# A batch's 6080 tokens cut into pairs of chunks of 512 and 504, in place of 512 and 480

## The chip, the cores and the metric

The kernel runs on one core of one Trainium2 chip. The metric is the device time of one execution in microseconds (us). The core has a matrix engine (TensorE, PE in the profile, with its weight loads as PEld), a vector engine (VectorE, DVE), an activation engine (ScalarE, ACT), GpSimd (POOL), and SyncE (SP), from whose queue all transfers are issued here.

## The reference

```python
def _attn_ref(q, k, v, tau):            # (4, 6080, 256) each
    qn = q / (np.linalg.norm(q, axis=1, keepdims=True) + 1e-06)
    kn = k / (np.linalg.norm(k, axis=1, keepdims=True) + 1e-06)
    s = kn.transpose(0, 2, 1) @ qn / tau
    s = s - s.max(-1, keepdims=True)
    a = np.exp(s)
    a /= a.sum(-1, keepdims=True) + 1e-09
    return v @ a

def _moe_ref(x, w_in, w_out):           # (24320, 256), (256, 2048), (2048, 256)
    h = x @ w_in
    g = h - np.tanh(h)
    return g @ w_out
```

The attention is over channels: for each of 4 batches a 256 x 256 matrix `a` is made from all 6080 tokens, and `v @ a` goes through a two-layer network with 2048 hidden units. All is float32.

## The kernel before, in words

**Folding.** Since `(v @ a) @ w_in = v @ (a @ w_in)`, the kernel multiplies `a` into `w_in` once a batch, and then streams the tokens of `v` through the folded weights `f`. A slot is one slice of 256 hidden units (there are 8 slices, `NS2`) against one pair of token chunks. The batch's tokens are cut into 6 pairs (L255 to L260): a pair takes `2 * n` tokens, `n` for each of its two chunks, with `n` at most 512 (`NMAX`). That gives five pairs of n = 512 and a last one of n = 480. A batch has 48 slots, and the 4 batches have 192.

**A slot.** Two chunks by two halves of the channels by two halves of the slice make a 2 x 2 block product, which is done in Strassen's way with 7 products, p1 to p7 (`Quad`, L965), into the PSUM banks x, y and z. Each number is held as a high part in float32r and a low part, and each product is three matmuls, high by low, high by high, low by high (`products`, L294 to L304; the matmul is at L300). So a slot has 21 matmuls of n columns here. ScalarE copies intermediate sums out (u, p at L999), VectorE adds them (c at L1015), and `finish` makes `h - tanh(h)` and splits it: tanh on ScalarE (L1027), the subtraction on VectorE (L1031), the high part gh on ScalarE (L1035), the low part gl on VectorE (L1039).

**The second layer.** `second` (L1077) multiplies each of the slot's four blocks by `w_out` in 6 matmuls (L1099), 24 in a slot, adding up over the 8 slices into the banks ps_o. After a pair's last slice the sums are copied out (ob, L1118) and stored (L1121).

**Beside it.** While one batch streams, the next batch's scores are built up from float32r matmuls of 256 columns (ps_s), in the batch's second to fifth pair; in its last pair come the softmax, and the fold of `a` into `w_in`, whose matmuls have 512 columns (x and z from wt). The first batch has its own scores, softmax and fold ahead, up to about 79 us. `Moving` (L775) loads a pair's tokens (vraw, L788), forms the sums that Strassen's products need (L795, L798) and splits them into high and low parts (L807, L810). These tiles are allotted at the full 512 whatever `n` is.

**What sets the order.** `Plan` (L85) collects all operations with costs in us and dependencies, and `order` places them: TensorE's in the order in which they were added, the others' by earliest start, then due time. The cost of a matmul is `pe_cost(n)` = 0.0134 + 0.000417 n. The outer loop (L1360) walks the slots and adds their products by the table `ORDER`; the second layer's matmuls are drawn from a stream that lags some 30 matmuls behind (`LAG`, `drain`, L1344). The host lays out the tokens pair by pair in the same cut (L1416 to L1419).

Of the kernel before, what the change touches and what calls it, by code (L numbers as in the profile page):

```python
# [18 lines left out]
P = 128  # L19
GJ = 2  # L20
NMAX = 512
NSQ = 760
F64_SCALE = 2.0 ** -112

# [210 lines left out]
def pe_cost(n):  # L235
    return 0.0134 + n * 0.000417


@with_exitstack
def attn_moe(ctx: ExitStack, tc: tile.TileContext, qk, v4, qkT, tau, w_in, w_out, outT):  # L240

# [6 lines left out]
    B, N, _, C = qk.shape  # L248
# [3 lines left out]
    FB = 2 * P  # L252
    NJ = N // P
    TAIL = N - NJ * P
    pairs = []  # L255
    s0 = 0
    while s0 < N:
        n = min(NMAX, (N - s0) // 2)
        pairs.append((s0, n))
        s0 += 2 * n  # L260
    NP = len(pairs)
    SLOTS = NP * NS2
    TOTAL = B * SLOTS
# [18 lines left out]
    def sb(pool, tag, shape, dtype, name):  # L282
        return pool.tile(list(shape), dtype, tag=tag, name=name, bufs=ring[tag].bufs)

    def bank(i, name, shape=(P, 512)):

        return ps_p.tile(list(shape), F32, tag=f"bank{i}", name=name)
# [38 lines left out]
    class Convert:  # L326
# [10 lines left out]
        def magnitude(self):  # L337
            words = self.raw.rearrange("p a (n w) -> p (a n) w", w=2)
            self.low, self.high = words[:, :, 0], words[:, :, 1]
            self.a = sb(nt_p, "nt", [P, NSQ], I32, f"a_{self.name}")[:, 0:WN]  # L340
            self.af = self.a.bitcast(F32)
# [98 lines left out]
    while j < NJ:  # L440
        n = min(GJ, NJ - j) if j else NJ % GJ or GJ
# [7 lines left out]
    class Attn:  # L449
# [26 lines left out]
        def square_plain(self, g):  # L476
            j0, n, rows = groups[g]
            raw = self.parts[g]
            if g == 0:

                self.acc = [bank(i, f"acc{i}_{self.b}", (P, 2, C)) for i in (4, 3)]
                self.acc.append(sb(g_p, "t", [P, NMAX], F32, "acc").rearrange("p (x c) -> p x c", x=2))
                for a in self.acc[n:]:
# [41 lines left out]
        def split_hi(self, g):  # L525
            j0, n, rows = groups[g]
            raw = self.parts[g][0]
            hi = sb(qk_p, "qh", [P, GJ, 2, C], F32R, f"qh_{self.b}_{g}")
            nc.scalar.copy(hi[:rows, 0:n], raw[:rows, 0:n])
            self.parts[g] = [hi, raw]  # L530
# [26 lines left out]
        def load_channels(self, i):  # L557

            row, part = divmod(i, N // NSQ)
            self.channels[i] = sb(nt_p, "nt", [P, NSQ], F32, f"nt_{self.b}_{i}")  # L560
            nc.sync.dma_start(
                self.channels[i],
                qkT[row // KC, self.b, row % KC * P:(row % KC + 1) * P, part * NSQ:(part + 1) * NSQ],
            )

        def square(self, i):
            if i == 0:
                self.squares = sm_p.tile([P, 2 * KC, N // NSQ], F32, name="squares")
            x = self.channels.pop(i)
            row, part = divmod(i, N // NSQ)  # L570
            nc.scalar.activation(x, x, AF.Square, accum_out=self.squares[:, row, part:part + 1])
# [203 lines left out]
    class Moving:  # L775
# [9 lines left out]
        def load(self):  # L785
            n, s0 = self.n, self.s0
            self.raw = sb(v_p, "vraw", [P, 4, NMAX], F32, f"vraw_{self.b}_{self.p}")
            nc.sync.dma_start(self.raw[:, :, 0:n], v4[self.b, :, 2 * s0:2 * s0 + 4 * n].rearrange("p (a n) -> p a n", a=4))  # L788

        def sums(self, i):  # L790
            n = self.n
            r = self.raw[:, :, 0:n]
            if i == 0:
                self.t = sb(v_p, "vt", [P, 4, NMAX], F32, f"vt_{self.b}_{self.p}")
                nc.vector.tensor_sub(self.t[:, 0:2, 0:n], r[:, 1:3, :], r[:, 0:2, :])  # L795
# [8 lines left out]
        def split_hi(self, i):  # L804
            x = sb(v_p, "vhl", [P, 2, NMAX], F32R, f"v{i}_{self.b}_{self.p}")
            self.hi[i], self.lo[i] = (x[:, j, 0:self.n] for j in range(2))
# [52 lines left out]
    def plan_product(b, q, p, z):  # L859
# [10 lines left out]
        ps = a.banks[to]  # L870
        plan.add("PE", 3 * pe_cost(NMAX), lambda to=to: a.fold_product(q, to, z, i, x, first), reads=[fbufs.pop((b, q, x)), a.ebuf] + [a.shbuf] * (i >= S1), writes=[ps])

# [487 lines left out]
    for gs in range(TOTAL):  # L1360
# [3 lines left out]
        for name, then in ORDER:  # L1364
# [6 lines left out]
            for x in then:  # L1371
                if isinstance(x, int):
                    lag, x = max(0, lag - x), max(0, x - lag)
# [68 lines left out]
```

## Time and profile before

| what | value |
|---|---|
| time, median of 3 runs | 2155.19 us (2155.01 to 2155.44) |
| span of the profiled execution, first to last instruction | 2154.0 us |
| instructions | 28464 |
| moved by DMA | 357.97 MB, mean 166 GB/s |

The profile gives the profiled execution by its span alone; it lies 1.2 us below the median, which also holds what is around the span. Four views are used. The page has the busy time of each engine and the chain of work that ended last. The groups list instructions of one line, operation and shape, with their number, busy time and mean duration of one; behind the last bar stand the engine's idle time just before them and what ended it. The timeline has one row for each run of like instructions: start in us, time from the first start to the last end, engine, line, tiles, shape and number. The windows give, for a stretch of time, its length and then the busy time and number of instructions of PE, PEld, DVE, ACT and POOL, the granted clock, and the DMA's share and rate.

Matmuls are pipelined: a matmul's duration in a row reaches past the start of the next one, so that TensorE's rate is read from the distance between starts.

### The profile page before, as it was taken

The numbers are of one execution on the slowest core, as the hardware profiler recorded it, in microseconds if no ns is written. First come the engines' busy times: TensorE is split into PE (matmuls) and PEld (weight loads), VectorE is DVE, ScalarE is ACT, GpSimd is POOL, SyncE is SP. The second block draws the span as 40 slices with busy tenths as digits, with TensorE's granted clock in tenths as the row PEclk, the third lists the DMA queues.
The fourth block names the chain that finished last, engine by engine and source line by source line (L and its number), as shares of the span: only waits on it lengthen the run. The fifth ranks groups of instructions, "written<-read, shape, count | busy, mean of one in ns | idle before, by whom it ended". The sixth has DMA issues, their size and how long they took to land.

```text
span 2154.0 us, 28464 instructions
## 1 busy us (share of the span) xinstructions
PE 2147.9 (100%) x9908; PEld 1805.5 (84%) x9908; DVE 1780.1 (83%) x2928; ACT 1540.0 (71%) x2762; POOL 34.8 (2%) x31
## 2 busy tenths in 40 slices
PE   9999999999999999999999999999999999999999
PEld 8888888888888888888888888888888888888888
DVE  8998878878888778787889877878788978778776
ACT  6677777767777777776777877777677766666665
POOL 5100000000000000000000000000000000000000
PEclk9999999999999999999999999999999999999999
DMA  9845556535335454543533555454353332332331
GB/s 382 304 162 203 187 208 217 181 128 183 133 134 201 164 206 168 209 160 111 193 137 124 187 193 206 145 215 166 107 193 129 142 131 88 140 125 86 131 115 53
DMA packets 97505, 357.97 MB, mean 166 GB/s; under 512 B 9938, under 2 KB 27346, under 8 KB 94802
## 3 DMA queue, kind: packets, MB, share of 16 engines
q1 hardware_dynamic: 97362, 356.16, 45.9%
q8 instruction: 78, 1.28, 0.2%
q14 instruction: 65, 0.53, 0.1%
HBM read 293.47 MB, written 62.65 MB: 165 GB/s over the span
## 4 chain that ended last, share of the span: by engine, by line
PE 99%; DMA 0%; SPq 0%; ACT 0%; issue 0%
PE ps_o L1099 48%; PE x L300 25%; PE y L300 12%; PE ps_s L300 7%; PE z L300 7%; PE ps_w L300 1%; DMA vhl<-qk_dram 0%; PE ps_b L613 0%; PE ps_t L648 0%; SPq L514 0%; SPq L335 0%; PE ps_n L506 0%; ACT ob L1118 0%; SPq L1291 0%; PE ps_tau L316 0%
## 5 line engine op out<-in xcount | busy, mean ns | idle before, releaser
L300 PE MATMUL x<-v,f 128*128 128x512 f32 (+1 forms) x2304 | 613.4, 388 | 0.0
L1099 PE MATMUL ps_o<-gh,wo_h 128*128 128x512 f32 (+1 forms) x1536 | 596.0, 388 | 0.0
L1099 PE MATMUL ps_o<-gh,wo_l 128*128 128x512 f32 (+1 forms) x1536 | 595.4, 388 | 0.0
L1039 DVE TENSOR_TENSOR gl<-t,gh 128x512 fp32r<-128x512 f32 (+1 forms) x768 | 510.2, 681 | 99.9 <-ACT gh L1035 94.2
L1035 ACT CAST gh<-t 128x512 fp32r<-128x512 f32 (+1 forms) x768 | 461.0, 617 | 125.4 <-DVE t L1031 110.0
L300 PEld LDWEIGHTS x<-v,f 128*128 128x128 f32 x2304 | 432.5, 188 | 87.0
L1027 ACT ACTIVATE t<-c 128x512 f32<-128x512 f32 (+1 forms) x576 | 361.5, 628 | 162.4 <-DVE c L1015 156.4
L1099 PE MATMUL ps_o<-gl,wo_h 128*128 128x512 f32 (+1 forms) x1536 | 471.6, 388 | 0.0
L1031 DVE TENSOR_TENSOR t<-c,t 128x512 f32<-128x512 f32 (+1 forms) x576 | 392.0, 682 | 94.8 <-ACT t L1027 87.8
L1099 PEld LDWEIGHTS ps_o<-gl,wo_h 128*128 128x128 f32 x1536 | 288.3, 188 | 57.9
L1099 PEld LDWEIGHTS ps_o<-gh,wo_l 128*128 128x128 f32 x1536 | 288.5, 188 | 55.7
L1099 PEld LDWEIGHTS ps_o<-gh,wo_h 128*128 128x128 f32 x1536 | 288.5, 188 | 55.5
L300 PE MATMUL y<-v,f 128*128 128x512 f32 (+1 forms) x1152 | 321.7, 387 | 0.0
L999 ACT COPY u<-x 128x512 f32<-128x512 f32 (+1 forms) x384 | 223.4, 582 | 128.5 <-PE x L300 125.7
L1015 DVE TENSOR_TENSOR c<-u,y 128x512 f32<-128x512 f32 (+1 forms) x384 | 260.0, 677 | 35.7 <-PE y L300 21.3
L300 PEld LDWEIGHTS y<-v,f 128*128 128x128 f32 x1152 | 216.2, 188 | 43.4
L1027 ACT ACTIVATE t<-x 128x512 f32<-128x512 f32 (+1 forms) x192 | 113.7, 592 | 111.8 <-PE x L300 111.1
L1031 DVE TENSOR_TENSOR t<-x,t 128x512 f32<-128x512 f32 (+1 forms) x192 | 131.2, 683 | 61.0 <-ACT t L1027 60.6
L1015 DVE TENSOR_TENSOR c<-p,z 128x512 f32<-128x512 f32 (+1 forms) x192 | 130.4, 679 | 37.1 <-PE z L300 34.4
L300 PE MATMUL z<-v,f 128*128 128x512 f32 (+1 forms) x576 | 160.8, 387 | 0.0
L300 PEld LDWEIGHTS z<-v,f 128*128 128x128 f32 x576 | 108.1, 188 | 21.6
L999 ACT COPY p<-x 128x512 f32<-128x512 f32 (+1 forms) x192 | 111.6, 581 | 3.0 <-PE x L300 0.9
(161 smaller groups left out, 1516.7 us busy)
## 6 DMA issues: line engine op xcount, KB each, us to landing
f<-f_d SPq DMA_DIRECT2D x160, 896.0 KB, 4.6
nt<-qkT_dram SPq DMA_DIRECT2D x96, 380.0 KB, 5.8
f_d<-f SPq DMA_DIRECT2D x32, 896.0 KB, 4.0
raw<-qk_dram SPq DMA_DIRECT2D x52, 512.0 KB, 5.8
vraw<-v_dram SPq DMA_DIRECT2D x20, 1024.0 KB, 7.8
outT_dram<-ob SPq DMA_DIRECT2D x80, 256.0 KB, 4.2
wt<-wt_d SPq DMA_DIRECT2D x24, 512.0 KB, 6.7
wt<-wi_d SPq DMA_DIRECT2D x36, 256.0 KB, 5.1
```

Of the source, the lines that this page charges most:

```text
L300: ins = nc.tensor.matmul(out, w, x, start=first and i == 0, stop=last and i == len(seq) - 1, skip_group_check=True,)
L999: nc.scalar.copy(self.tiles[to], self.tiles["X"][:, 0:self.n])
L1015: nc.vector.tensor_add(self.tiles[i], self.tiles[u], self.tiles[ps][:, 0:self.n])
L1027: nc.scalar.activation(self.tiles["t", i], self.tiles[c][:, 0:n], AF.Tanh)
L1031: nc.vector.tensor_sub(x, self.tiles[c][:, 0:n], x)
L1035: nc.scalar.copy(self.g[i][0], self.tiles["t", i])
L1039: nc.vector.tensor_sub(self.g[i][1], self.tiles["t", i], self.g[i][0].bitcast(F32))
L1099: nc.tensor.matmul(outs[key + (m,)][:, 0:n], (wo_l if part else wo_h)[:, f, m * P:(m + 1) * P], quad.g[i][x], start=first and j == 0, stop ...
```

## The change

The loop that cut off 512 after 512 is replaced by a function that divides a batch's tokens as evenly as steps of 8 allow, with the same number of pairs. For 6080 tokens: `count` = 6, `each` = 63, `more` = 2, so two pairs of n = 64 x 8 = 512 and four of n = 63 x 8 = 504. The host uses the same function for its layout.

```diff
+UNIT = 8
...
+def token_pairs(N):
+
+    count = -(-N // (2 * NMAX))
+    each, more = divmod(N // (2 * UNIT), count)
+    pairs = []
+    s0 = 0
+    for p in range(count):
+        n = UNIT * (each + (p < more))
+        pairs.append((s0, n))
+        s0 += 2 * n
+    assert s0 == N and pairs[0][1] <= NMAX
+    return pairs
...
-    pairs = []
-    s0 = 0
-    while s0 < N:
-        n = min(NMAX, (N - s0) // 2)
-        pairs.append((s0, n))
-        s0 += 2 * n
+    pairs = token_pairs(N)
...
-    for s0 in range(0, N, 2 * NMAX):
-        x, y = np.split(vT[:, :, s0:s0 + 2 * NMAX], 2, axis=2)
+    for s0, n in token_pairs(N):
+        x, y = np.split(vT[:, :, s0:s0 + 2 * n], 2, axis=2)
```

The lines of the changed kernel are 10 further down (L300 becomes L310, L1099 becomes L1109). On TensorE, in the last batch's fifth pair (x, y of pair 4, slices 6 and 7, with the second layer of slice 5), before:

```order
L300 MATMUL x_4_6_20299<-v_3_4_19712,f_20151 128x512 x3
L300 MATMUL x_4_7_20389<-v_3_4_19357,f_20246 128x512 x3
L1099 MATMUL ps_o_4_1_1_19923<-gh_3_4_5_20313,wo_h 128x512
L300 MATMUL y_4_6_20353<-v_3_4_19739,f_20151 128x512 x3
L1099 MATMUL ps_o_4_1_1_19923<-gl_3_4_5_20324,wo_h 128x512
L1099 MATMUL ps_o_4_1_0_19918<-gl_3_4_5_20324,wo_h 128x512
```

and at the same place now:

```order
L310 MATMUL x_4_6_20299<-v_3_4_19712,f_20151 128x504 x3
L310 MATMUL x_4_7_20389<-v_3_4_19357,f_20246 128x504 x3
L1109 MATMUL ps_o_4_1_1_19923<-gh_3_4_5_20313,wo_h 128x504
L310 MATMUL y_4_6_20353<-v_3_4_19739,f_20151 128x504 x3
L1109 MATMUL ps_o_4_1_1_19923<-gl_3_4_5_20324,wo_h 128x504
L1109 MATMUL ps_o_4_1_0_19918<-gl_3_4_5_20324,wo_h 128x504
```

Only the number of columns differs, and so it is over the whole of TensorE's program, 6822 rows in both. On ScalarE, in the first batch's third pair (pair 2, slices 2 and 3; p, u, t and gh as above, nt the squares for the next batch's norms), before:

```order
L1027 ACTIVATE t_0_2_2_2816<-x_2_2_2701 128x512
L571 ACTIVATE nt_14_2765,squares<-nt_14_2765 128x760
L999 COPY p_0_2_3_2826<-x_2_3_2812 128x512
L1035 CAST gh_0_2_2_2832<-t_0_2_2_2810 128x512
L1035 CAST gh_0_2_2_2838<-t_0_2_2_2816 128x512
```

and now:

```order
L1037 ACTIVATE t_0_2_2_2816<-x_2_2_2701 128x504
L1009 COPY p_0_2_3_2823<-x_2_3_2812 128x504
L581 ACTIVATE nt_14_2765,squares<-nt_14_2765 128x760
L1045 CAST gh_0_2_2_2833<-t_0_2_2_2810 128x504
L1045 CAST gh_0_2_2_2838<-t_0_2_2_2816 128x504
```

The copy of p and the squares have changed places. Such swaps of neighbours are found in ScalarE's, VectorE's and SyncE's programs from the third pair on.

## The prediction

> **What bounds the kernel now.** I read the page from the top: busy shares, then the chain that ended last, then the granted clock.
>
> ```profile
> PE 2147.9 (100%) x9908; PEld 1805.5 (84%) x9908; DVE 1780.1 (83%) x2928; ACT 1540.0 (71%) x2762; POOL 34.8 (2%) x31
> PE 99%; DMA 0%; SPq 0%; ACT 0%; issue 0%
> core 0: 2154.0 us, clock 1.000
> ```
>
> TensorE is the chain from end to end, at a full granted clock. The other engines wait for it, not it for them. So the time is the sum of the spacings from one matmul's start to the next one's, and the question is what one matmul of 504 columns costs. A matmul's own duration in the groups (about 390 ns) does not say it, because matmuls overlap; the spacing has to be taken from the timeline.
>
> The work comes in slots: one pair of chunks against one 256-wide slice of the hidden layer. By the code a slot has 7 products of 3 matmuls and 24 matmuls of the second layer, 45 in all. The groups kept apart by shape bear that out for the sixth pair (4 batches x 8 slots = 32 slots):
>
> ```profile
> L300 PE MATMUL x<-v,f 128*128 128x480 f32 x384 | 99.4, 378 | 0.0
> L1099 PE MATMUL ps_o<-gh,wo_h 128*128 128x480 f32 x256 | 97.2, 380 | 0.0
> L1099 PE MATMUL ps_o<-gh,wo_l 128*128 128x480 f32 x256 | 96.6, 377 | 0.0
> L1099 PE MATMUL ps_o<-gl,wo_h 128*128 128x480 f32 x256 | 76.5, 379 | 0.0
> L300 PE MATMUL y<-v,f 128*128 128x480 f32 x192 | 51.9, 378 | 0.0
> L300 PE MATMUL z<-v,f 128*128 128x480 f32 x96 | 26.0, 379 | 0.0
> ```
>
> They add up to 1440 = 32 x 45, and the last column says that TensorE was never idle ahead of one. A slot's period can be read off its z product, which comes once a slot. In the last batch, where nothing else is inserted, TensorE's timeline has it at these starts (first column, us), six slots apart at 512 columns and four slots apart at 480:
>
> ```profile
> 1709.59 0.84 PE L300 MATMUL z<-v,f 128*128 128x512 f32 x3
> ...
> 1770.79 0.84 PE L300 MATMUL z<-v,f 128*128 128x512 f32 x3
> ...
> 2086.48 0.81 PE L300 MATMUL z<-v,f 128*128 128x480 f32 x3
> ...
> 2125.48 0.81 PE L300 MATMUL z<-v,f 128*128 128x480 f32 x3
> ```
>
> At 512 a slot takes 61.20 / 6 = 10.20 us, at 480 it takes 39.00 / 4 = 9.75 us. Divided by 45, a matmul starts every **226.7 ns** at 512 columns and every **216.7 ns** at 480. A third size stands in the scores of the earlier batches, 256 columns:
>
> ```profile
> 1003.81 0.28 PE L300 MATMUL ps_s<-ql,qh 128*128 128x256 f32 x1
> 1003.93 0.28 PE L300 MATMUL ps_s<-qh 128*128 128x256 f32 x1
> 1004.05 0.28 PE L300 MATMUL ps_s<-qh,ql 128*128 128x256 f32 x1
> 1004.17 0.40 PE L1099 MATMUL ps_o<-gh,wo_l 128*128 128x512 f32 x1
> ```
>
> Three in 0.36 us, so 120 ns each. These three sizes do not lie on a line. From 256 to 512 the price is 106.7 ns for 256 columns, 0.4167 ns a column, and 13.3 ns a matmul beside it. On that line 480 columns would cost 213.3 ns and a slot 9.60 us; the trace has 9.75. **The 480 size pays 3.3 ns a matmul, 0.15 us a slot, above the line that 256 and 512 lie on.** Everything hangs on whether 504 pays that too.
>
> **The change, part by part.** Columns are conserved: a batch's halves are 5 x 512 + 480 = 3040 before and 2 x 512 + 4 x 504 = 3040 now. The number of matmuls, of slots and of instructions on every engine stays, and TensorE's order stays row for row apart from the sizes. Per run that is 24 pairs x 8 = 192 slots. Before, 160 of them are 512 and 32 are 480: 160 x 10.20 + 32 x 9.75 = 1944.0 us. Now 64 are 512 and 128 are 504: 652.8 + 128 x s, with s the slot at 504. So the change costs nothing at s = 1291.2 / 128 = 10.0875 us, and each 0.01 us of s is worth 1.28 us.
>
> No row of this trace has 504 columns, so s is bounded from both sides. Lower end: the line through 256 and 512 gives 226.67 - 8 x 0.4167 = 223.33 ns, s = 10.05 us, and the change saves 128 x 0.0375 = **4.8 us**. Middle: the line through 480 and 512, the two nearest sizes, gives 224.2 ns, s = 10.0875 us, and by construction exactly **nothing**. Upper ends: if 504 pays what 480 pays, 223.33 + 3.33 = 226.67 ns, s = 10.20 us, the same slot as at 512, and the change costs 128 x 0.1125 = **14.4 us**. If it pays more, the dearest run of spacings that I find without a wait is that of 512-column matmuls just behind three of 480:
>
> ```profile
> 502.31 0.40 PE L1099 MATMUL ps_o<-gh,wo_h 128*128 128x512 f32 x1
> ...
> 504.39 0.39 PE L1099 MATMUL ps_o<-gh,wo_h 128*128 128x512 f32 x1
> ```
>
> Nine matmuls of 512 stand in those 2.08 us, 231.1 ns each, 4.4 ns above their settled 226.7. With 4.4 ns on the line 504 would cost 227.8 ns, s = 10.25 us, and the change 20.7 us.
>
> I take 14.4 us, for what these rows say about the kind of price. The sizes 256 and 512 settle into an even beat; 480 does not:
>
> ```profile
> 1100.27 0.37 PE L1099 MATMUL ps_o<-gh,wo_l 128*128 128x480 f32 x1
> 1100.48 0.38 PE L1099 MATMUL ps_o<-gh,wo_h 128*128 128x480 f32 x1
> 1100.70 0.37 PE L1099 MATMUL ps_o<-gh,wo_l 128*128 128x480 f32 x1
> 1100.91 0.38 PE L1099 MATMUL ps_o<-gh,wo_h 128*128 128x480 f32 x1
> 1101.13 0.59 PE L1099 MATMUL ps_o<-gl,wo_h 128*128 128x480 f32 x2
> ```
>
> The spacings alternate, 0.21 and 0.22 us: every second one stands on the line, and the next pays for both. Behind an odd number of 480s (three, above) the following 512s are late for some nine matmuls. Behind an even number they are not:
>
> ```profile
> 505.07 0.81 PE L300 MATMUL x<-v,f 128*128 128x480 f32 x3
> 505.72 0.82 PE L300 MATMUL z<-v,f 128*128 128x480 f32 x3
> 506.38 0.39 PE L1099 MATMUL ps_o<-gh,wo_l 128*128 128x512 f32 x1
> ...
> 507.28 0.81 PE L300 MATMUL y<-v,f 128*128 128x480 f32 x3
> ```
>
> Six of 480, then four of 512 in 0.90 us, 225 ns each, settled at once. Something keeps step with the columns, 512 and 256 leave it in step, and 480 puts it half out and then back in. 504 is as little in step with 512 or 256 as 480 is, so I expect it to pay on average, and the nearest measured average is 480's 3.3 ns. That step, from 480 to 504, is the weak one.
>
> The other terms are small. Slots in which two sizes are mixed cost a little more than their parts:
>
> ```profile
> 2066.57 0.81 PE L300 MATMUL z<-v,f 128*128 128x480 f32 x3
> ...
> 2076.65 0.81 PE L300 MATMUL z<-v,f 128*128 128x480 f32 x3
> ```
>
> This slot takes 10.08 us, where 21 matmuls of 480 and 24 of 512 would make 21 x 0.2167 + 24 x 0.2267 = 9.99. Before and now there are seven such changes of size (one within each batch, one between batches), with two mixed slots each at most; at 0.09 us that is 7 x 0.18 = 1.3 us, which I leave where it is and keep as a margin either way. VectorE and ScalarE follow the columns:
>
> ```profile
> L1118 ACT COPY ob<-ps_o 128x512 f32<-128x512 f32 x40 | 23.4, 586 | 7.3 <-PE ps_o L1099 6.6 <-DMA outT_dram<-ob 0.5
> L1118 ACT COPY ob<-ps_o 128x480 f32<-128x480 f32 x8 | 4.5, 559 | 4.4 <-PE ps_o L1099 4.3
> 520.00:583.00 63.00, 63.00 (x293) 54.24 (x292) 52.47 (x102) 43.35 (x79) 0.00 (x0) 1.00 0.51 180
> 90.00:176.00 86.00, 86.00 (x409) 72.34 (x408) 84.39 (x152) 65.53 (x121) 3.27 (x2) 1.00 0.50 185
> ACT v L807 <- DMA vraw<-v_dram: 1.7, 1, 1.7
> ```
>
> The copy that ends the program grows by 27 x 24/32 = 20 ns, the only certain gain or loss behind the last matmul. In the sixth pair (second-to-last window row, the columns being length, then PE, PEld, DVE, ACT) VectorE is busy 52.5 of 63 us; its operations there grow by 5%, about 2.6 us, under cover of the 10.5 us that it is idle. The one stretch where VectorE has no slack, 84.4 of 86 us, is the first pair of the first batch, which stays at 512. The new tokens were waited for once, 1.7 us at the start; the loads shrink or grow by at most 5%. Swaps in ScalarE's and SyncE's order are between neighbours. I cost all this at nothing; were TensorE made to wait 0.1 us in each of the 128 slots, it would be 12.8 us.
>
> **Sum.** The profiled execution has a span of 2154.0 us, 1.2 us below the median of 2155.19; I carry that difference over. 2154.0 + 14.4 = 2168.4 us of span, **2169.6 us** of time, 0.7% slower.
>
> **Rivals.** *The straight line holds (faster).* 480's 3.3 ns would then be no matter of step but a floor under the spacing, near 216.7 ns, that 512 and now 504 clear. It decides from the point where the line passes the floor, (216.7 - 13.3) / 0.4167 = 488 columns: 504 is above it, so s = 10.05 us and the time is 2155.2 - 4.8 = 2150.4 us. For it: 480 keeps about the same mean in two batches, 0.86 us for the four spacings that alternate above and 216.7 ns each in the last pair. Against it: the 256s above run at 120 ns, well under such a floor; and 512s behind an odd number of 480s, which are far above it, are late all the same. The Trainium skill, on the page "TensorE: Matmul & The Clock Gate", section "Back-to-back issue gap", gives N / 2.4 + 2.5 ns for warm matmuls, a straight line with the same slope. By that rule's slope 504 costs 223.3 ns, as in this rival; its own figures, 215.8 ns at 512 and 202.5 ns at 480, lie 11 and 14 ns below this trace, and its excess being unequal at the two sizes is where the trace disagrees.
>
> *The excess fades with nearness to 512 (no change).* With 480 and 512 as the ends of one line, 504 pays a quarter of 480's excess, 0.8 ns, and the time stays at 2155.2 us. For it: nearest neighbours; against it: that 256 is on 512's line.
>
> *The change does nothing but rename sizes* is excluded by the order of the instructions: 504 stands there in 128 of 192 slots.
>
> **How the numbers follow.** 504 out of step, 14.4 us and up to 20.7: 0.48. The straight line: 0.34. Fading excess: 0.18. A measurement of this kernel tells about 0.2%, 4.3 us, from no change. The first case is slower in 0.46, and within 0.2% in 0.02 if the excess is a third of what I take. The straight line's 4.8 us is just beyond the bound, and the margin of 1.3 us goes both ways: 0.22 faster, 0.12 the same. The fading one: 0.02 faster, 0.13 the same, 0.03 slower. That makes 0.24 faster, 0.27 the same, 0.49 slower. Both signs hold much of the chance, so the range takes in all three: from 2150.4 - 1.3 = 2149.1 to 2155.2 + 20.7 + 1.3 = 2177.2 us. The likeliest case's own range is 2162 to 2177.
>
> **What would show it.** In the changed profile, z starts of a pair of 504 in the last batch: 10.20 us apart for my forecast, 10.05 for the straight line, 10.09 for the fading one. Spacings of 504 should be uneven, as those of 480 were, and 512s mixed among them should be late. The slots of 512 must stay at 10.20 and TensorE's idle time at nothing ahead of the product and output matmuls. I am wrong if 504 settles into an even beat near 223.3 ns, or if VectorE or a transfer comes up as what TensorE waits for.

## The result, and the profile after

The changed kernel takes 2170.07 us (median, 2169.97 to 2170.48) where the kernel before, run beside it, takes 2155.40 us. The ratio is 1.0069, with a 95% interval of 1.0057 to 1.0081: slower by 14.7 us. Forecast were 2169.6 us and 14.4 us. The profiled execution has a span of 2168.2 us, 14.2 more than before.

The page of the changed kernel, its busy shares and its chain, and the answer on the clock:

```profile
PE 2163.1 (100%) x9908; PEld 1807.0 (83%) x9908; DVE 1778.4 (82%) x2928; ACT 1541.3 (71%) x2762; POOL 35.4 (2%) x31
PE 99%; DMA 0%; SPq 0%; ACT 0%; issue 0%
core 0: 2168.2 us, clock 1.000
```

As many matmuls as before, at the same clock, and TensorE is still the whole chain. Its busy time grew by 15.2 us, while VectorE's fell by 1.7. So the time went into the matmuls' spacing. The timeline of TensorE in the last batch gives it by the starts of the z products, one a slot (the rows come in couples, three or four slots apart):

```profile
1720.17 0.84 PE L310 MATMUL z<-v,f 128*128 128x512 f32 x3
...
1750.77 0.84 PE L310 MATMUL z<-v,f 128*128 128x512 f32 x3
...
1914.14 0.84 PE L310 MATMUL z<-v,f 128*128 128x504 f32 x3
...
1954.94 0.84 PE L310 MATMUL z<-v,f 128*128 128x504 f32 x3
...
2087.54 0.84 PE L310 MATMUL z<-v,f 128*128 128x504 f32 x3
...
2128.34 0.84 PE L310 MATMUL z<-v,f 128*128 128x504 f32 x3
```

Three slots of 512 take 30.60 us; four of 504 take 40.80 us, in the fourth pair and again in the sixth. All are 10.20 us, 226.7 ns a matmul. **Where no other size is mixed in, a matmul of 504 columns costs exactly what one of 512 costs.** There, shrinking a chunk from 512 to 504 saves nothing, and growing one from 480 to 504 costs all of the 0.45 us a slot.

The same reading for each pair of both traces, as the distance of its first z start from the next pair's, divided by its 8 slots (7 for the last pair of all), in us a slot, worked out from the timelines:

```
batch         pair 1   pair 2   pair 3   pair 4   pair 5   pair 6
1   before    10.708   10.683   10.565   10.565   10.400   10.563
1   after     10.708   10.687   10.578   10.560   10.398   10.977
2,3 before    10.680   11.205   11.477   11.477   11.130   10.562
2,3 after     10.741   11.209   11.478   11.460   11.118   10.977
4   before    10.680   10.200   10.200   10.200   10.197    9.809
4   after     10.741   10.204   10.217   10.200   10.200   10.200
```

Pairs 3 to 5 went from 512 to 504 and did not move by more than 0.02 us, whether scores are made beside them (batches 1 to 3) or not. Pair 6 went from 480 to 504: 24 slots x 0.415 + 8 x 0.391 = 13.1 us. Pair 1 of batches 2 to 4 stayed at 512, but the second layer's lag brings the last pair's matmuls into it: 24 x 0.061 = 1.5 us. Together 14.6, against 14.2 in the span. The rest lies ahead of the slots: the first z product starts at 81.85 us instead of 82.35, since TensorE waited 0.4 us for the first loads where it had waited 1.4.

The two sums share the sixth pair's matmuls. Counted in the trace, 324 of such a pair's 360 start between its first z and that of the next batch, 30 behind that, and 6 ahead. At 10 ns each, 3.24 and 0.30 us were due in the two distances; 8 x 0.415 = 3.32 and 8 x 0.061 = 0.49 us were measured. So the sixth pair paid its whole price, and mixing the sizes cost another 0.27 us at each of the three batch changes.

### The profile page after: what moved, and what is told of

Its sections match the earlier page's. It is cut to its first block, busy times and chain, and to the rows that moved or that the text cites. A ratio compares the mean times of both kernels' runs of the same rounds, so it can differ in the third digit from the quotient of the medians.

```text
span 2168.2 us, 28482 instructions
## 1 busy us (share of the span) xinstructions
PE 2163.1 (100%) x9908; PEld 1807.0 (83%) x9908; DVE 1778.4 (82%) x2928; ACT 1541.3 (71%) x2762; POOL 35.4 (2%) x31
## 4 chain that ended last, share of the span: by engine, by line
PE 99%; DMA 0%; SPq 0%; ACT 0%; issue 0%
PE ps_o L1109 48%; PE x L310 25%; PE y L310 12%; PE ps_s L310 7%; PE z L310 7%; PE ps_w L310 1%; DMA vhl<-qk_dram 0%; PE ps_b L623 0%; PE ps_t L658 0%; SPq L524 0%; PE ps_n L516 0%; ACT ob L1128 0%; SPq L345 0%; SPq L1301 0%; PE ps_tau L326 0%
## 5 line engine op out<-in xcount | busy, mean ns | idle before, releaser
L310 PE MATMUL x<-v,f 128*128 128x504 f32 (+1 forms) x2304 | 617.1, 389 | 0.0
L1109 PE MATMUL ps_o<-gh,wo_h 128*128 128x504 f32 (+1 forms) x1536 | 598.0, 389 | 0.0
L1109 PE MATMUL ps_o<-gh,wo_l 128*128 128x504 f32 (+1 forms) x1536 | 597.7, 389 | 0.0
L1049 DVE TENSOR_TENSOR gl<-t,gh 128x504 fp32r<-128x504 f32 (+1 forms) x768 | 509.9, 680 | 93.0 <-ACT gh L1045 86.8
L1045 ACT CAST gh<-t 128x504 fp32r<-128x504 f32 (+1 forms) x768 | 460.8, 617 | 111.3 <-DVE t L1041 96.1
L310 PEld LDWEIGHTS x<-v,f 128*128 128x128 f32 x2304 | 432.6, 188 | 90.2
L1037 ACT ACTIVATE t<-c 128x504 f32<-128x504 f32 (+1 forms) x576 | 361.6, 628 | 169.1 <-DVE c L1025 163.3
L1109 PE MATMUL ps_o<-gl,wo_h 128*128 128x504 f32 (+1 forms) x1536 | 473.5, 389 | 0.0
L1041 DVE TENSOR_TENSOR t<-c,t 128x504 f32<-128x504 f32 (+1 forms) x576 | 391.4, 681 | 89.7 <-ACT t L1037 81.6
L1109 PEld LDWEIGHTS ps_o<-gl,wo_h 128*128 128x128 f32 x1536 | 288.5, 188 | 59.8
L1109 PEld LDWEIGHTS ps_o<-gh,wo_l 128*128 128x128 f32 x1536 | 288.6, 188 | 58.5
L1109 PEld LDWEIGHTS ps_o<-gh,wo_h 128*128 128x128 f32 x1536 | 288.6, 188 | 57.6
L1009 ACT COPY u<-x 128x504 f32<-128x504 f32 (+1 forms) x384 | 223.3, 581 | 145.2 <-PE x L310 142.0
L310 PE MATMUL y<-v,f 128*128 128x504 f32 (+1 forms) x1152 | 323.7, 389 | 0.0
L1025 DVE TENSOR_TENSOR c<-u,y 128x504 f32<-128x504 f32 (+1 forms) x384 | 259.8, 676 | 48.2 <-ACT u L1009 26.3
L310 PEld LDWEIGHTS y<-v,f 128*128 128x128 f32 x1152 | 216.3, 188 | 45.2
L310 PE MATMUL z<-v,f 128*128 128x504 f32 (+1 forms) x576 | 161.7, 389 | 0.0
L310 PEld LDWEIGHTS z<-v,f 128*128 128x128 f32 x576 | 108.1, 188 | 22.7
```

What stands on the lines that cost most here:

```text
L310: ins = nc.tensor.matmul(out, w, x, start=first and i == 0, stop=last and i == len(seq) - 1, skip_group_check=True,)
L1009: nc.scalar.copy(self.tiles[to], self.tiles["X"][:, 0:self.n])
L1025: nc.vector.tensor_add(self.tiles[i], self.tiles[u], self.tiles[ps][:, 0:self.n])
L1037: nc.scalar.activation(self.tiles["t", i], self.tiles[c][:, 0:n], AF.Tanh)
L1041: nc.vector.tensor_sub(x, self.tiles[c][:, 0:n], x)
L1045: nc.scalar.copy(self.g[i][0], self.tiles["t", i])
```

## The experiments

The theory was that the excess of 3.3 ns, which 480 pays above the line of 256 and 512, belongs to the size of a float32r matmul itself, and that 504 pays it too. Its rivals were that it comes from something in the kernel: other engines, the weights, the place of a size in the order, what precedes it. Streams of matmuls alone answer the first part, other cuts of the tokens the second.

**Streams alone.** The first kernel has nothing but matmuls (`...` stands for lines left out, here and below):

```diff
+    def block(name, at, cols):
+        for n in SIZES:
...
+            for t, k in ((a, LEAD), (b, COUNT)):
+                for i in range(k):
...
+                    nc.tensor.matmul(
+                        ps[j % 2][0:cols, 0:n], w[:, j * 128:j * 128 + cols], t[:, at:at + n],
...
+    block("whole", 0, 128)
+    block("half", 0, 64)
+    block("offset", 8, 128)
```

> This kernel computes none of the reference: it streams matmuls of one float32r operand over rotating 128 x 128 float32r weights, 32 and then 64 of each of 20 sizes, first whole, then with weights of 64 columns, then with the moving operand 8 columns further in. The spacing of the 64 is read from the timeline. Theory 1 (step): 512, 448, 384, 320 and 256, the multiples of 64, lie on the line of 0.4167 ns a column + 13.3 ns (226.7, 200.0, 173.3, 146.7, 120.0), and every other size lies 3.3 ns above it (504: 226.7, 496: 223.3, 480: 216.7, 464: 210.0, 416: 190.0). Theory 2 (treads): columns are taken in blocks and a begun block is paid whole, so 504 costs what 512 costs and the sizes between stand on flat treads (500, 504, 508 and 512 all 226.7; 488 and 496 alike). Theory 3 (only this kernel): with nothing else running all sizes lie on the line, 504 at 223.3 and 480 at 213.3. If the fixed 13.3 ns is the load of the weights taking turns with the columns, weights of 64 columns bring it to about 6.7 ns; if not, it stays. The offset of 8 columns should change nothing if the length alone counts.

TensorE's timeline; the spacing of the 64 is the next row's start less the row's own, divided by 64. The last two couples are 504 with weights of 64 columns, and 500 with the operand 8 columns further in:

```profile
59.30 14.67 PE L42 MATMUL ps<-b,w 128*128 128x504 f32 x64
73.81 7.31 PE L42 MATMUL ps<-a,w 128*128 128x500 f32 x32
...
102.39 14.46 PE L42 MATMUL ps<-b,w 128*128 128x496 f32 x64
116.69 7.20 PE L42 MATMUL ps<-a,w 128*128 128x488 f32 x32
123.72 14.24 PE L42 MATMUL ps<-b,w 128*128 128x488 f32 x64
137.80 7.09 PE L42 MATMUL ps<-a,w 128*128 128x480 f32 x32
144.74 14.03 PE L42 MATMUL ps<-b,w 128*128 128x480 f32 x64
158.60 6.98 PE L42 MATMUL ps<-a,w 128*128 128x472 f32 x32
165.43 13.82 PE L42 MATMUL ps<-b,w 128*128 128x472 f32 x64
179.08 6.85 PE L42 MATMUL ps<-a,w 128*128 128x464 f32 x32
...
225.66 13.13 PE L42 MATMUL ps<-b,w 128*128 128x448 f32 x64
238.63 6.57 PE L42 MATMUL ps<-a,w 128*128 128x440 f32 x32
...
300.48 11.68 PE L42 MATMUL ps<-b,w 128*128 128x400 f32 x64
312.00 5.73 PE L42 MATMUL ps<-a,w 128*128 128x384 f32 x32
...
433.36 14.92 PE L42 MATMUL ps<-b,w 128*64 128x504 f32 x64
448.12 7.25 PE L42 MATMUL ps<-a,w 128*64 128x500 f32 x32
...
783.89 14.67 PE L42 MATMUL ps<-b,w 128*128 128x500 f32 x64
798.40 7.34 PE L42 MATMUL ps<-a,w 128*128 128x496 f32 x32
```

With nothing beside it, 504 takes 226.7 ns and 480 takes 216.6, as in the kernel. So the other engines, the transfers and the kernel's order are not the cause, and theory 3 is out. From 472 to 504, in steps of 8, the first pass bears out what the forecast took over from 480: 213.3, 216.6, 220.0, 223.4 and 226.7 ns, all some 16.7 ns beyond 0.4167 ns a column, where 512 has 13.3. As a rule for all sizes the step theory falls: 448, a multiple of 64, lies at 202.7 where the line has 200.0, and 400, which is none, lies on it at 180.0. Theory 2 is out too: 500 came at 223.3, not at the 226.7 of 504 and 512, and 496 and 488 differ.

Weights of 64 columns did not halve the fixed part: 480 stayed at 216.6, 384 and 320 at 173.4 and 146.7. But they were not without effect: 256 fell from 120.0 to 113.3 and 500 from 223.3 to 220.0, while 504 rose to 230.6 and 512 to 230.2. With the operand 8 columns further in, 504 stayed at 226.7, but 500 rose from 223.3 to 226.7 and 416 from 188.3 to 193.3. So the length alone does not settle the price of every size.

**What the excess depends on.** Two more streams, one that puts foreign matmuls between and ends with bfloat16, one that varies the weights and the rows:

```diff
+    for n in SIZES:
+        for m in KICKS:
+            for k in KICK_COUNTS:
+                run(w, a, m, k)
+                run(w, b, n, SETTLE)
+                run(w, c, n, COUNT)
+    for n in (512, 508, 504, 500, 496, 488, 480, 472, 464, 456, 448, 400, 384, 256):
+        run(hw, ha, n, SETTLE)
+        run(hw, hc, n, COUNT)
```

> Leaves out the reference altogether: a stream of float32r matmuls of one size (512, 504, 496 or 480), into which 1, 2 or 3 matmuls of another size (64 to 448 columns) are put; then 32 to settle and 48 that are read from the timeline. At its end a bfloat16 stream of 14 sizes. Price theory: each size has one price whatever came before: 512 226.7, 504 226.7, 496 223.3, 480 216.7 ns after every kick. Beat theory: a size can settle in more than one beat and what came before chooses: after some kicks 496 comes at 220.0 and 504 at 223.3, after others at 223.3 and 226.7; 512 comes back to 226.7 after all. If the excess belongs to the 4-byte columns, bfloat16 lies on one line over all sizes; if it belongs to any stream with new weights each time, 504 and 480 lie above the line of 512 and 256 there too.

From its timeline, first 496 after two of the kicks, then bfloat16; the last two lines are from its groups and show the weight loads of both kinds:

```profile
1266.66 10.88 PE L41 MATMUL ps<-c,w 128*128 128x496 f32 x48
...
1284.63 10.72 PE L41 MATMUL ps<-c,w 128*128 128x496 f32 x48
...
1796.13 10.36 PE L41 MATMUL ps<-hc,hw 128*128 128x504 bf16 x48
1806.33 6.91 PE L41 MATMUL ps<-ha,hw 128*128 128x500 bf16 x32
...
1862.88 9.88 PE L41 MATMUL ps<-hc,hw 128*128 128x480 bf16 x48
1872.60 6.54 PE L41 MATMUL ps<-ha,hw 128*128 128x472 bf16 x32
...
L41 PEld LDWEIGHTS ps<-c,w 128*128 128x128 f32 x4608 | 865.2, 188 | 163.8
L41 PEld LDWEIGHTS <-hw 128*128 128x128 bf16 x1120 | 109.6, 98 | 105.6 <-issue 0.2
```

504 and 512 came at 226.7 after all 24 kicks each. 496 has two beats: 48 of them last 10.88 us after 23 kicks (223.3 ns a spacing) and 10.72 after one, a single matmul of 448 (220.0, on the line). 480 came at 216.7 each time. So a size can settle in more than one beat; 504 showed one. In bfloat16, 504 takes 10.20 / 48 = 212.5 ns and 480 takes 202.5: 10 ns for 24 columns, with 2.5 ns beside the columns. Here a weight load took 98 ns, against 188 in float32r. The spacing is the formula that the Trainium skill, page "TensorE: Matmul & The Clock Gate", section "Back-to-back issue gap", gives for warm matmuls (N / 2.4 + 2.5 ns); it holds for this stream, and for the kernel's float32r it is 14 ns short at 504 and at 480.

```diff
+    for n in SIZES:
+        run(w, b, n, SETTLE)
+        run(w, c, n, COUNT)
+    for n in SIZES:
+        run(w, b, n, SETTLE, loads=1)
+        run(w, c, n, COUNT, loads=1)
+    for n in SIZES:
+        run(w, b, n, SETTLE, rows=64)
+        run(w, c, n, COUNT, rows=64)
+    for n in SIZES:
+        run(wf, bf, n, SETTLE)
+        run(wf, cf, n, COUNT)
```

> Leaves out the reference: streams of eight sizes, 48 of each read, four times over: float32r with four weight tiles in turn (as in the kernel), float32r with the same weights every time, float32r with 64 of the 128 rows, and plain float32. First block, as in the sweep and the kicks: 512 226.7, 504 226.7, 496 223.3, 488 220.0, 480 216.7, 400 180.0, 256 120.0. Theory weights: the excess comes from new weights between the columns; with the same weights every time all sizes fall onto one line. Theory length: nothing changes with the weights, 504 still costs what 512 costs. Theory rows: with half of the rows the excess halves. Plain float32, which takes a column in several passes: an even line, as bfloat16 had.

From its timeline, 504 with four weights, with one (and that pass's weight loads), with 64 rows, and in plain float32:

```profile
35.89 11.04 PE L37 MATMUL ps<-c,w 128*128 128x504 f32 x48
46.77 7.31 PE L37 MATMUL ps<-b,w 128*128 128x496 f32 x32
...
164.98 10.84 PEld L37 LDWEIGHTS ps<-c,w 128*128 128x128 f32 x48
165.20 11.04 PE L37 MATMUL ps<-c,w 128*128 128x504 f32 x48
176.08 7.31 PE L37 MATMUL ps<-b,w 128*128 128x496 f32 x32
...
294.71 11.04 PE L37 MATMUL ps<-c,w 64*128 64x504 f32 x48
305.59 7.30 PE L37 MATMUL ps<-b,w 64*128 64x496 f32 x32
...
494.50 40.72 PE L37 MATMUL ps<-c,w 128*128 128x504 f32 x96
535.06 26.78 PE L37 MATMUL ps<-b,w 128*128 128x496 f32 x64
```

10.88 / 48 = 226.7 ns three times over: neither different weights nor the number of rows matter to 504. But with one weight tile there were still 48 loads to 48 matmuls, as the PEld row shows. So the theory of the weights was tested only for their being new: no run leaves the loads out, and since weights of 64 columns did change spacings, the load stays a possible part of the excess. Plain float32, which the trace shows as two passes, takes 40.56 / 96 = 422.5 ns a pass, and its 512 takes 429.2: 6.7 ns less for 8 columns, 2.5 ns beside 0.8333 ns a column at both. Of the three types tried, float32r alone has the uneven prices.

**Size by size.** The last stream takes every fourth size. It is the first pass of the stream before, with another list (the edit is shown against that kernel):

```diff
-SIZES = [512, 504, 496, 488, 480, 448, 400, 256]
+SIZES = list(range(512, 252, -4))
```

> Leaves out the reference: float32r streams of every size from 512 down to 256 in steps of 4, 32 to settle and 48 read. The sizes read before should come again: 512 226.7, 504 226.7, 496 223.3 (or 220.0), 480 216.7, 400 180.0, 384 173.3, 320 146.7, 256 120.0. Regular theory: the excess over the line repeats with a fixed period in the columns, so that the sizes on the line can be named by a rule (say every 64 or every 128, which 448 at 202.7, 2.7 ns above the line, already speaks against). Irregular theory: neighbours differ by up to 5 ns with no period, and only a measured table tells which size is cheap. No size comes below the line through 256 and 512 by more than 0.5 ns.

```profile
52.88 11.04 PE L37 MATMUL ps<-c,w 128*128 128x504 f32 x48
63.76 7.31 PE L37 MATMUL ps<-b,w 128*128 128x500 f32 x32
70.90 10.88 PE L37 MATMUL ps<-c,w 128*128 128x500 f32 x48
81.62 7.31 PE L37 MATMUL ps<-b,w 128*128 128x496 f32 x32
...
176.99 10.40 PE L37 MATMUL ps<-c,w 128*128 128x476 f32 x48
187.23 6.98 PE L37 MATMUL ps<-b,w 128*128 128x472 f32 x32
194.05 10.40 PE L37 MATMUL ps<-c,w 128*128 128x472 f32 x48
204.29 6.93 PE L37 MATMUL ps<-b,w 128*128 128x468 f32 x32
```

Spacings worked out from such rows, in ns, good to about 0.2:

```
512 226.7   508 227.5   504 226.7   500 223.3   496 223.3   492 222.3
488 225.6   484 218.8   480 216.7   476 213.3   472 213.3   468 211.7
448 202.5   444 200.0   440 200.0   436 193.3   400 180.0   384 173.3
```

The irregular theory held, but not wholly: there are treads, on which sizes close together share a spacing (500 and 496, 476 and 472, 444 and 440; also 512 and 504, but not 508 between them), and the shared values are whole multiples of 3.33 ns (67, 64, 60 and 68 of them). 34 of the 65 sizes lie within 0.1 ns of such a multiple; the others do not. Some settled in uneven spacings, such as 488, which repeats a cycle of seven from 221 to 241 ns with a mean of 225.6 here, although it came evenly at 220.0 in the first and the third stream. The expectation that nothing lies below the line was a miss: 436 is 1.7 ns below, and so are 292 (133.3) and other sizes near 300. A reason why the spacing takes such steps was not found.

**Other cuts in the kernel.** All leave the computation whole. In `token_pairs` a list takes the place of the division. First two pairs of 496 at the end:

```diff
...
-    for p in range(count):
-        n = UNIT * (each + (p < more))
+    for n in [512, 512, 512, 512, 496, 496]:
```

> Pairs of 512, 512, 512, 512, 496, 496. Slots before: 1944.0 us. Step theory: 496 pays 206.7 + 13.3 + 3.3 = 223.3 ns, 10.05 us a slot: 128 x 10.20 + 64 x 10.05 = 1948.8, so 4.8 us slower than before, about 2160. Treads of 8 or more with 496 whole: 220.0 ns, 9.90 us, 1939.2, so 4.8 us faster, about 2150.5. If 496 rounds up to 512: 1958.4, 14.4 us slower.

2154.81 us against 2155.55, ratio 0.9997 (0.9987 to 1.0007): no change, between two expectations. Its trace shows both beats of 496; in the last pair of the last batch the z starts are

```profile
2064.22 0.82 PE L307 MATMUL z<-v,f 128*128 128x496 f32 x3
...
2103.82 0.82 PE L307 MATMUL z<-v,f 128*128 128x496 f32 x3
```

four slots in 39.60 us, 9.90 a slot or 220.0 ns, while over the whole run the spacing after a 496 is 222.3 ns in the mean: where scores or fold are mixed in, in the first three batches, it is some 223 ns, and 220.0 in the last.

Then one pair of 504, with 488 to make up the sum:

```diff
...
-    for p in range(count):
-        n = UNIT * (each + (p < more))
+    for n in [512, 512, 512, 512, 504, 488]:
```

> Pairs of 512 x 4, 504, 488: one pair of 504 in place of four. If the sizes keep the spacing of the sweep (504 226.7, 488 220.0 ns: 10.20 and 9.90 us a slot) the slots make 160 x 10.20 + 32 x 9.90 = 1948.8 us, 4.8 slower than before, about 2160.3. If both lay on the line (10.05, 9.75): 1939.2, 4.8 faster. If both lay on the line from 480 to 512: 1944.0, no change.

2164.76 against 2155.57 us, ratio 1.0043 (1.0028 to 1.0058): 9.2 us slower, where the sweep's spacings gave 4.8. The sign held and both lines are out. The rest is in the slots. 488 beside the fold takes 10.80 us, 0.24 more than 480 there, where 0.15 was due (24 x 0.09 = 2.2 us). The 504 beside the scores of batches 2 and 3, and the first pair of the next batch, take 0.05 more in 16 and 24 slots (2.0 us). Over the run the spacing after a 488 is 222.3 ns in the mean, between its 220.0 and its 225.6 in the streams. In this mixture, a stream of one size told too little.

Then the changed kernel's sizes in the other order:

```diff
...
-    for p in range(count):
-        n = UNIT * (each + (p < more))
+    for n in [504, 504, 504, 504, 512, 512]:
```

> The changed kernel's sizes in the other order: four pairs of 504, then two of 512. If a 504 costs what a 512 costs wherever it stands: 192 x 10.20 = 1958.4 us of slots, 14.4 slower than before, the same time as the changed kernel within 1.3 us. If the price of 504 came from what precedes it (512s, or the scores' 256s), the pairs of 504 ahead of and beside the scores take another slot than 10.20 us, down to 10.05: up to 19 us less.

2169.67 us, ratio to before 1.0066 (1.0049 to 1.0083), 0.4 us from the changed kernel. In the second pair of the last batch, now of 504, the z starts are four slots apart in these rows:

```profile
1760.39 0.84 PE L307 MATMUL z<-v,f 128*128 128x504 f32 x3
...
1801.19 0.84 PE L307 MATMUL z<-v,f 128*128 128x504 f32 x3
```

That is 10.20 us a slot again, and 512, now in the sixth pair beside the fold, has 10.945, where 504 had 10.977. So neither the place nor the neighbours make 504's price, though among the fold's 512s it pays about 0.03 us a slot more.

Last the sizes of before with the 480 elsewhere, in the first pair and, in another kernel, in the fifth (`[512, 512, 512, 512, 480, 512]`):

```diff
...
-    for p in range(count):
-        n = UNIT * (each + (p < more))
+    for n in [480, 512, 512, 512, 512, 512]:
```

> The same sizes as before, the 480 moved from the last pair to the first. If a size has its spacing wherever it stands: the same 1944.0 us of slots, no change within 1.3. If 480 loses its beat beside the fold's 512-column products, which fill the last pair (10.56 us a slot before, against 10.98 with 504 there, a difference of 0.41 where 0.45 is due): 24 slots x 0.04 = 0.9 us faster.

> The same sizes as before, the 480 moved from the last pair to the fifth, beside the scores' 256-column matmuls and between two pairs of 512. Spacing by size alone: no change. If mixing sizes has a price, one more change of size in the last batch and none less: 0.2 us slower there, and the gain of up to 0.9 us of the fold's pair.

2155.56 us, ratio 0.9999 (0.9990 to 1.0009), and 2156.38, ratio 1.0004 (0.9994 to 1.0013), against 2155.42: no change either way. The small gain that the fold's pair might have brought did not appear. It had been read from 0.41 us a slot where 0.45 was due, and that gap is the tenth of the pair's matmuls that starts outside the distance measured, not a cheaper 480. No cut that was run beats the kernel before beyond its uncertainty.

## Why the prediction was right

- *TensorE's spacing is the time.* Held: same number of matmuls, same clock, and the slots add up to 14.6 us where the span grew by 14.2, with 0.5 us less ahead of them. VectorE, ScalarE and the transfers stayed under cover, as costed; new tokens were waited for once, 2.3 us at the start. The 1.2 us carried over from span to time was a small error: every run that has both numbers takes 1.7 to 1.9 us more than its own span, so the profiled execution of before lay some 0.6 us above the median.
- *512 columns stay at 10.20 us a slot.* Held in the last batch, apart from its first pair.
- *504 costs 10.20 us a slot.* Held to the last digit where no other size is mixed in. It was the weak step: 480's 3.3 ns above the line were carried over to 504. In the first stream 472 to 504, in steps of 8, all pay them, so the transfer between neighbours was sound; that it would be was not known, and a little further the excess differs (464, 208.9 ns, has 2.2 above the line, and 456, 209.0, has 5.7).
- *The margin for mixed slots, 1.3 us either way.* It was enough: from the first z product to the last matmul the time grew by 14.7 us (2067.6 to 2082.3), 0.3 more than the sum. The 13.1 us of the sixth pair and the 1.5 us of the first pair behind it are no two effects, as the matmuls of one pair are spread over both. The 0.27 us of mixing at each change of batch, 0.8 in all, were in part made up elsewhere. They are in the main 512s late among 504s, as forecast: the 348 in such a first pair took 0.19 us more than at 226.7 ns each, against 0.04 before.
- *The picture behind it failed.* I expected 504 out of step, with uneven spacings. It settles into an even beat, the same as 512's. The reason given, that 512 and 256 leave something in step and other sizes put it out, would have 504 uneven; 400 is as even as they are, at 180.0 on the line, and 504 is even 3.3 ns above it. In its place the runs show that about half of the sizes stand on multiples of 3.33 ns, 504 and 512 on the same one, and not why. The number came out right because the sum took over only the mean excess; that it did not hang on the uneven beat was luck.
- *The straight line* is refuted (504 at 226.7, not 223.3), and so is the floor on which it rested: 476, 472 and smaller sizes run well under 216.7 ns. *The fading excess* is refuted too: 508, nearer to 512, is dearer than 512.

## What to carry to other kernels

Where matmuls of one kind fill the time, cutting the same columns more evenly is not neutral: the price of a size must be measured, in a stream of a few dozen of that size, since in float32r 8 columns can cost nothing (512 and 504) or 6.7 ns (444 and 436). Read it from the distance between starts, over a whole period of the loop, not from durations. Then leave the sizes that pay most beyond their columns in as few slots as possible, as one pair of 480 does here, and measure the mixture as well: the pair of 504 and the pair of 488 cost 4.4 us, 0.2%, more than the streams said.

## What the runs showed of the hardware

- Float32r matmuls are spaced 13.3 ns apart beyond their columns at 512 and 256, and 11.7 to 22.3 in the sizes of the table above; bfloat16 2.5 ns at 504, 496 and 480, and plain float32 2.5 ns a pass at 512, 504 and 448 beyond 0.8333 ns a column.
- 504 kept its 226.7 ns with four weight tiles or one, 128 rows or 64, starting column 0 or 8, and with all other engines idle; with weights of 64 columns it took 230.6. 500 took 223.3 ns, and 226.7 with the operand 8 columns further in.
- 496 has two stable beats, 220.0 and 223.3 ns: 220.0 after one of 24 kicks, and in the last batch of the kernel with two pairs of 496.
- A weight load stands beside every float32r matmul of the streams, the same weights or not, and no run shows the spacing without it. Why the spacing goes in steps is open.
